# Threshold attention and an ELU feed-forward: the first 45 attention steps as one list of timed jobs

## The chip, the core and the metric

The kernel runs on one core of a Trainium2 chip. The metric is the device time of one execution in microseconds; the kernel before takes 1319.03 us (median of 3 runs, 1318.7 to 1320.56). Everything is float32. The engines are named as in the profile: PE (TensorE), DVE (VectorE), ACT (ScalarE), POOL (GpSimd), SP (the queue that issues most DMAs). Each engine runs its own instructions in the order in which the program emits them; a semaphore holds an instruction back until its inputs are there and the buffer that it writes is free. So the order of emission, engine by engine, is the schedule, and it is what this change alters.

## The reference

```python
# q, k, v: (8, 8, 576, 64); tau = 0.02; w_in (512, 2048); w_out (2048, 512)
scores = q @ k.T / 8
thresh = max(scores, axis=-1) - tau
scores = where(scores >= thresh, scores, -1e9)
attn = softmax(scores)
x = (attn @ v).transpose(0, 2, 1, 3).reshape(4608, 512)
h = x @ w_in
g = where(h > 0, h, exp(min(h, 0)) - 1)
out = g @ w_out
```

## The kernel before

**Steps.** Attention is done in pairs of heads: 32 pairs (4 to a batch entry). A pair has five steps, `steps[n] = (pr, i)`: i = 0 to 3 are 128 query rows of both heads, i = 4 (`NC`) is the last 64 rows of both heads in one tile. A step computes scores on PE (L283), the negated row maximum on DVE (L293, L321), a threshold on POOL (L325), the exponential on ACT (L335), the masked product with its row sum on DVE (L344), sum and reciprocal on DVE (L350, L351), and the normalized weights `w` on POOL (L317). The weights are then turned, so that keys lie on partitions: either by PE transposes (L354) and ACT copies (L370), in three parts (nine transposes of 128x128; six where i = 4), or "in squares": DVE transposes 32x32 blocks (L428), and two DMAs by way of DRAM put the blocks in place (L457, and `fetch`, L465). After i = 1 and after i = 4 the product with v follows (`values`, L489 and L494) and a copy of it (`values_out`, L611).

**Three loops.** The change concerns steps 0 to 44. They are emitted by three loops, in which the order is written out by hand.

- Loop 1 (L780), steps 0 to 19. PSUM holds three score tiles of one head each (two banks each) and two single banks (`t`). A step's transposes are emitted within the next step, and scores of the next step before its own second mask. Dummy transposes of the identity (`spare`, L374, counts at L793 and L825) are put ahead of the real ones. Six 512-column pieces of the feed-forward's weights are converted on the way from a double-width integer form: each needs a shift (DVE, L167), an add (POOL, L176), two activations (ACT, L156, L181) and a product (DVE, L189). In all there are 32 pieces.
- Loop 2 (L874), steps 20 to 34, with new PSUM pools: two score tiles, two banks for the feed-forward (`f`), two for `t`. Two pieces of weights are converted in each step until all are there. The feed-forward of the first 512 tokens (two chunks c of 256) is put between, in halves: a half is four matmuls, which the trace shows as eight instructions of 256 columns (`ffn1`, L652) or four of 512 columns (`ffn2_plain`, L692). A unit of `ffn1` (two halves, one bank) is followed by an exponential (ACT, L659), a subtraction (POOL, L662) and a product (DVE, L666), after which its bank is free. `SHARES` (L868) says how many halves a step takes at four points. A unit is taken only when the weight pieces that it needs are converted (`needs`, L731). The units are pushed at the end of step 21 (L949), so the first halves are emitted in step 22. After step 34 the loop turns that step's weights on PE, finishes the open unit and the open values (L953 to L956).
- Loop 3 (L1046), steps 35 to 44, with new PSUM pools again: three banks for `f`, two score tiles, one bank for `t` (L960). Here all weights are turned in squares, the halves are given by `QUOTA` (L1041), and DVE and POOL also prepare sums of the weight blocks for what follows. The SBUF pool of the early stage (`wstage`) is closed first and its space reused (`late`).

After step 44 comes the rest of the kernel, from pair 9 on: attention in wider PSUM tiles together with a feed-forward that uses fewer products (L541, L588 to L601, L1149, L1289), ordered by an agenda of jobs with times (`at`, `until`, L1098 to L1116), in which the table `MOVED` (L19) adds an offset in microseconds to a job's time. That agenda sorts the emission only; nothing on the chip waits for such a time. The rest of the kernel is not changed, except for where its three `f` banks are allocated.

The lines that decide loop 2's turning and banks, for reference:

```python
for name, bufs in (("s", 2), ("f", 2)):
...
    SHARES = ((1, 1, 1, 1), (0, 1, 1, 0), (1, 1, 1, 0), (0, 1, 1, 0), (1, 1, 1, 0))
...
            if steps[n - 2] == (NPAIR - 1, NB - 1):
                push_ffn(0)
...
        turn(*steps[SWITCH - 1])
        finish_units(ffn_halves(len(pending)), ALL)
        behind(*steps[SWITCH - 2])
        behind(*steps[SWITCH - 1])
```

Of the kernel before, what the change touches and what calls it, by code (L numbers as in the profile page):

```python
# [19 lines left out]
    'f0.0': -2.08, 'f1.0': -0.13, 'f1.1': 0.2, 'f10.0': 0.05, 'f11.0': -0.04, 'f12.1': 0.12, 'f13.1': -0.5,  # L20
    'f14.0': 0.02, 'f15.1': -0.06, 'f16.0': 0.04, 'f16.1': 0.69, 'f16.2': -0.14, 'f17.0': -0.28, 'f18.1': 0.12,
    'f2.0': -5.54, 'f2.1': -0.25, 'f2.2': 0.7, 'f20.1': -1.03, 'f21.0': 0.13, 'f22.1': -0.19, 'f23.0': 0.08,
    'f23.1': 2.72, 'f23.2': 0.07, 'f25.0': 0.39, 'f26.0': -0.08, 'f26.1': 0.42, 'f3.0': 0.35, 'f5.0': -0.32,
    'f5.1': 4.32, 'f6.1': -0.54, 'f7.0': -0.01, 'f9.0': 0.35, 'f9.1': 1.94, 'fbound0': -0.14, 'fbound1': 0.93,
    'fbound4': -0.36, 'fe00': 0.1, 'fe10': 0.37, 'fe11': 0.3, 'fe20': -0.6, 'fexp00': 0.1, 'fexp20': 0.25,
    'fexp31': 0.12, 'ffetch0': 1.19, 'ffetch1': -0.24, 'ffetch2': -0.52, 'ffetch3': -0.65, 'fkcopy': -0.11,
    'floadk': -2.59, 'floadq': 2.51, 'fm00': -3.15, 'fm01': -0.49, 'fm11': -2.07, 'fm20': 1.6, 'fm21': -0.43,
    'fmask00': 1.48, 'fmask01': -0.63, 'fmask10': 0.68, 'fmask11': 0.02, 'fmask30': -0.16, 'fmask31': 0.36,
    'fmask4': 0.2, 'fmax00': -0.03, 'fmax01': -0.65, 'fmax10': 0.91, 'fmax11': 0.5, 'fmax20': -0.99,
    'fmax21': -0.15, 'fmax30': 0.04, 'fmax31': -0.17, 'fmax4': 0.36, 'fnorm01': 0.83, 'fnorm10': -0.23,  # L30
    'fnorm11': -0.44, 'fnorm20': 1.68, 'fnorm31': -0.75, 'fout1': 0.83, 'fsum0': 0.21, 'fsum2': 0.33,
    'fsum3': 0.21, 'fturn0': 0.21, 'fturn2': 0.46, 'fturn3': -1.27, 'fturn4': -3.36, 'fx0': -0.43, 'fx10': 3.03,
    'fx11': 2.86, 'fx2': 1.4, 'fx3': 0.53, 'fx6': -1.72, 'fx8': -0.33, 'fx9': 1.95, 's13.0': -0.93,
    's13.1': 0.11, 's13.2': 0.73, 's13.3': 1.36, 's15.1': -0.14, 's17.3': -1.92, 's19.0': 0.23, 's19.1': 1.66,
    's21.0': 0.22, 's23.0': 1.98, 's23.1': 4.28, 's23.2': 2.4, 's25.1': -0.53, 's25.2': 1.32, 's25.3': 0.43,
    's27.0': -2.01, 's3.0': -0.77, 's3.2': 0.37, 's5.0': -2.21, 's7.0': 0.39, 's9.0': -3.16, 's9.1': -0.03,
    'sbound0': 0.06, 'sbound1': 0.6, 'sbound3': 0.33, 'sbound4': -0.31, 'sexp00': 0.32, 'sexp01': -0.15,
    'sexp10': -0.99, 'sexp11': -0.09, 'sexp20': 0.5, 'sexp30': -1.71, 'sexp31': -0.33, 'sexp4': 0.82,
    'sfetch0': -0.75, 'sfetch3': -0.18, 'sfetch4': 0.31, 'sloadk': -1.81, 'sm31': 0.19, 'smask11': 0.49,
    'smask20': -0.39, 'smask21': -0.03, 'smask30': -0.19, 'smask31': 0.34, 'smax10': -4.94, 'smax11': -0.3,  # L40
    'smax20': 0.07, 'smax21': 0.74, 'smax30': 0.68, 'smax4': 0.21, 'snorm00': 0.1, 'snorm01': -0.01,
    'snorm10': 0.08, 'snorm21': -0.13, 'snorm30': 0.24, 'snorm31': 1.3, 'snorm40': 0.68, 'sout0': -1.7,
    'sout1': -0.49, 'sprep0': 0.21, 'sprep1': -0.32, 'ssum3': 0.21, 'ssum4': 0.35, 'sturn0': 1.44, 'sturn1': 0.3,
    'sturn2': -0.07, 'sturn3': 0.1, 'sturn4': -1.49, 'sx0': -0.87, 'sx1': -0.05, 'sx10': 0.8, 'sx11': -0.5,
    'sx2': -1.66, 'sx3': 0.47, 'sx4': -2.3, 'sx5': 1.3, 'sx6': 1.26, 'sx8': 4.1, 'sx9': -0.98,
# [4 lines left out]
def kernel(  # L50
# [85 lines left out]
    progress = [0, 0]  # L136

    def load_w(ahead=2):
        i = progress[0]
        if i >= len(pieces) or i >= progress[1] + ahead:  # L140
            return
        progress[0] += 1
        src, dst, j, n = pieces[i]
        rows = src[j * P : (j + 1) * P]
        if src.dtype == FP32:
            nc.sync.dma_start(dst, rows[:, n : n + WN])
            return
        st = staged[i] = wstage.tile([P, WN, 2], U32, name="wst", bufs=4)
        nc.sync.dma_start(st.rearrange("p n w -> p (n w)"), rows.bitcast(U32)[:, 2 * n : 2 * (n + WN)])
# [8 lines left out]
    def convert_top(i):  # L158
        convert_shift(i)
        convert_sign(i)  # L160


# [5 lines left out]

    def convert_sign(i):
        pass  # L170
# [13 lines left out]
    def convert_end(i):  # L184

        progress[1] = i + 1
        if i in staged:
            sign, top = staged.pop(i)[:, :, 1].bitcast(I32), tops.pop(i).bitcast(FP32)
            nc.vector.scalar_tensor_tensor(pieces[i][1], top, 0.0, sign, ALU.max, ALU.mult)  # L189
# [5 lines left out]
    def load(pr, parts=("qm", "km", "v"), shared=False, queue=nc.sync):  # L195
# [13 lines left out]
        if "v" not in parts:  # L209
            return  # L210
# [38 lines left out]
    spare = []  # L249
    e_both, e_next = att.tile([P, 2, 2, HALF], FP32, name="e", bufs=1), [0]  # L250
# [49 lines left out]
    def masks(pr, i, hs):  # L300
        st = open_steps[pr, i]
        cs = slice(hs[0], hs[-1] + 1)
        if hs[0] == 0:
            st["w"] = wpool[0].tile([P, 2 * S], FP32, name="w")
# [33 lines left out]
    def mask_of(pr, i, h):  # L338
        st = open_steps[pr, i]
        if h == 0:  # L340
            st["w"] = wpool[0].tile([P, 2 * S], FP32, name="w")
# [81 lines left out]
    def turn_squares(pr, i):  # L423
        w = open_steps.pop((pr, i))["w"]
        x = late["x"].tile([P, NT, NCH, T], FP32, name="x", bufs=2)
# [279 lines left out]
    def push_ffn(g):  # L705
        if g:
            return
        for c in range(PLAIN):
            units.extend((ffn1, (c, u)) for u in range(NU))
            units.extend((ffn2_plain, (c, i, p)) for p in range(NFT // 4) for i in range(2))  # L710
# [7 lines left out]
    def behind(pr, i):  # L718
        if i in (1, NB - 1):
            values(pr, 0 if i == 1 else 1)()  # L720
        if i == NB - 1 and (pr + 1) % NPAIR == 0 and pr + 1 < NP:
            push_ffn(pr // NPAIR)
# [13 lines left out]
    def ffn_halves(n):  # L736
        after = []
        while n and (pending or units):
            if not pending:
                if needs(*units[0]) > progress[1]:  # L740
                    break
# [14 lines left out]

    with tc.manual_schedule():
        load(0, ("qm",))  # L760
        nc.sync.dma_start(tau_sb, tau.to_broadcast([P, 1]))
        load(0, ("km",), queue=nc.scalar)
        load(0, ("v",))
        load(1)


        def idle(n):
            rt = psum["t"].tile([P, NC, P], FP32, name="rt", tag="rt")
            for _ in range(n):
                transpose(rt[:, 0], ident)  # L770

        idle(28)
        prep_q(0)
        prep_k(0)
        read_tau()
        copy_k(0)
        copy_q(0)
        scores(0, 0, [0, 1])
        out_values = None
        for n in range(per_seq):  # L780
            pr, i = steps[n]
            hs = heads_of(i)
            x = progress[1]
            if n:
                normalize(*steps[n - 1], [0])
                turned = turn_parts(*steps[n - 1])
            max_of(pr, i, 0)
            exp_of(pr, i, 0)
            bound_of(pr, i, 0)

            first_scores = n > 2 and i in (2, NB - 1)
            if n and not first_scores:
                spare.append(6 if pr else 9)  # L793
                copies = turned[0]()
            if len(hs) == 2:
                max_of(pr, i, 1)
            if n and len(heads_of(steps[n - 1][1])) == 2:
                normalize(*steps[n - 1], [1])
            if len(hs) == 2:
                exp_of(pr, i, 1)  # L800
                bound_of(pr, i, 1)
            if out_values:
                out_values()
            if n and not first_scores:
                copies()

            if i == NB - 1 and n + 1 < per_seq:
                convert_top(x)
                convert_add(x)
                convert_abs(x)  # L810
                convert_rest(x + 1)
            elif i == 0 and n:
                convert_end(x)
                load_w()
            elif i == 1 and pr:
                convert_sign(x)
                convert_add(x)
            elif i in (2, 3):
                (prep_q if i == 2 else prep_k)(pr + 1)
                if i == 2:  # L820
                    scale_q(pr + 1)
                (copy_q if i == 2 else copy_k)(pr + 1)
            mask_of(pr, i, 0)
            if n and not first_scores:
                spare.append(8 if pr else 11)  # L825
                turned[1]()()
            elif not n:
                idle(16)
            if n + 1 < per_seq:
                scores(*steps[n + 1], heads_of(steps[n + 1][1]))  # L830
            if n:
                for part in turned[0 if first_scores else 2 :]:
                    part()()
            if len(hs) == 2:
                mask_of(pr, i, 1)
            reciprocal_of(pr, i, hs)
# [33 lines left out]
    with tc.manual_schedule():  # L870
        carried = []
        for _ in range(2):
            load_w(4)
# [685 lines left out]
```

## Time and profile before

| | us |
|---|---|
| median of 3 runs | 1319.03 |
| profiled execution, its own time | 1320.34 |
| its span, first to last instruction | 1318.6 |
| PE busy in the span | 1298.9 |
| DVE, POOL, ACT busy in the span | 1012.1, 805.2, 559.5 |
| start of the scores of step 0 | 8.12 |
| start of the scores of step 20 | 98.34 |
| start of the scores of step 22 | 113.55 |
| start of the scores of step 35 | 220.22 |
| start of the scores of step 44 | 288.84 |
| first PE instruction of the rest (L588) | 296.2 |

The span is counted from the first instruction. Busy times of PE are modelled: a matmul that waits inside the pipeline counts as busy, so gaps are better seen between the starts of neighbouring matmuls. The granted clock is that of PE, 1.00 being full speed. In the chain of waits each row is a stretch of the chain that ended last, with its start, its length, and the engine and line that filled it; "issue" is time in which the engine waited for nothing that the profile shows.

### The profile page before, as it was taken

Reading aid. Unit: us, or ns where it says so; the run is one execution under the profiler, and the core shown is the slowest. Engines: PE = TensorE matmul, PEld = TensorE weight load, DVE = VectorE, ACT = ScalarE, POOL = GpSimd, SP = SyncE. Lnnn points to the kernel's source line nnn. Section 1 sums busy time; section 2 is a strip of 40 time slices with the busy share of each in tenths; the row PEclk is TensorE's granted clock in tenths of the full one; section 3 lists DMA queues with packets and bytes.
Section 4 is the critical chain, followed back from the end, with each engine's and each line's share of the span. In section 5 each row is a group of like instructions: output and inputs, shape, how many; then the busy total and the mean of one; then the engine's idle time right before and its main releaser. Section 6 shows DMA issues by size and latency. Waiting matters only on the chain.

```text
span 1318.6 us, 22013 instructions
## 1 busy us (share of the span) xinstructions
PE 1298.9 (99%) x6980; PEld 1011.0 (77%) x6980; DVE 1012.1 (77%) x2195; ACT 559.5 (42%) x1219; POOL 805.2 (61%) x1186
## 2 busy tenths in 40 slices
PE   8999999999999999999999999999999999999998
PEld 7666756647778777777878777878777787888886
DVE  6877775988888988898898979897889882545534
ACT  5676664225353444444443535252526250422320
POOL 4657774768657665767475747584768463624533
PEclk9998999999999999999999999999999999999999
DMA  6255452788897989898889888989889775221221
GB/s 120 61 107 161 136 143 57 220 241 241 222 257 221 259 214 245 214 260 232 240 216 256 239 234 224 259 240 245 234 235 258 216 214 185 93 72 60 93 60 32
DMA packets 322595, 247.76 MB, mean 188 GB/s; under 512 B 208688, under 2 KB 284464, under 8 KB 322480
## 3 DMA queue, kind: packets, MB, share of 16 engines
q1 hardware_dynamic: 320112, 246.07, 68.6%
q8 instruction: 55, 0.90, 0.3%
q10 hardware_dynamic: 2368, 0.30, 0.2%
q14 instruction: 60, 0.49, 0.1%
HBM read 161.81 MB, written 84.48 MB: 187 GB/s over the span
## 4 chain that ended last, share of the span: by engine, by line
PE 93%; DVE 3%; DMA 1%; ACT 1%; issue 1%; SPq 1%; POOL 0%; ACTq 0%; DVEq 0%
PE f L1289 29%; PE f L1149 28%; PE sc L541 8%; PE sc L601 7%; PE rt L354 4%; PE sc L283 4%; PE f L652 4%; PE f L692 3%; PE pv L494 3%; PE sc L593 1%; PE sc L588 1%; DMA there<-x 1%; PE pv L489 1%; DVE x L428 1%; SPq L457 0%
## 5 line engine op out<-in xcount | busy, mean ns | idle before, releaser
L317 POOL TENSOR_SCALAR w<-w,rs 128x576 f32<-128x576 f32 x196 | 169.1, 871 | 85.6 <-DVE rs L351 75.5
L548 DVE TENSOR_REDUCE mx<-sc 128x1 f32<-128x576 f32 x207 | 148.3, 750 | 35.3 <-PE sc L541 32.4
L558 ACT ACTIVATE w<-sc,mx 128x576 f32<-128x576 f32 x115 | 83.0, 740 | 114.6 <-DVE mx L548 96.8
L1149 PE MATMUL f<-xt,sw 128*128 128x256 f32 x512 | 123.8, 384 | 0.8 <-ACT xt L611 0.5
L1149 PE MATMUL f<-xt,w_in_sb 128*128 128x256 f32 x512 | 122.3, 381 | 0.3 <-ACT w L1163 0.3
L554 POOL TENSOR_SCALAR th<-mx,ntau 128x2 f32<-128x2 f32 (+1 forms) x115 | 34.3, 298 | 137.8 <-DVE mx L548 137.8
L1149 PEld LDWEIGHTS f<-xt,w_in_sb 128*128 128x128 f32 x512 | 96.1, 190 | 16.0 <-ACT w L1163 3.2
L1149 PEld LDWEIGHTS f<-xt,sw 128*128 128x128 f32 x512 | 93.7, 190 | 18.2 <-ACT xt L611 0.9
L541 PE MATMUL sc<-kT,qT 64*128 64x512 f32 (+4 forms) x736 | 107.5, 423 | 0.0
L1149 PE MATMUL f<-x,w_in_sb 128*128 128x256 f32 x448 | 106.1, 379 | 1.4 <-ACT g L1210 1.4
L1289 PE MATMUL f<-w_out_sb,g 128*128 128x256 f32 x448 | 107.1, 382 | 0.0
L541 PEld LDWEIGHTS sc<-kT,qT 64*128 64x128 f32 x736 | 80.8, 186 | 34.2 <-issue 16.8
L1289 PE MATMUL f<-w_out_sb,s 128*128 128x256 f32 x448 | 107.0, 382 | 0.0
L1289 PE MATMUL f<-t,s 128*128 128x256 f32 x448 | 105.8, 379 | 0.0
L428 DVE STREAM_TRANSPOSE x<-w 128x512 f32<-128x512 f32 (+2 forms) x143 | 96.6, 709 | 10.6 <-POOL w L317 10.3
L562 DVE SCALAR_TENSOR_TENSOR w<-sc,th,w 128x576 f32<-128x576 f32 x115 | 89.8, 811 | 11.4 <-ACT w L558 9.2
L1236 POOL TENSOR_TENSOR s<-g 128x256 f32<-128x256 f32 x104 | 80.4, 779 | 29.4 <-PE f L1289 20.1
L1149 PEld LDWEIGHTS f<-x,w_in_sb 128*128 128x128 f32 x448 | 85.0, 190 | 13.4 <-ACT g L1210 1.8
L1289 PEld LDWEIGHTS f<-w_out_sb,g 128*128 128x128 f32 x448 | 84.1, 190 | 12.9 <-issue 0.7
L1289 PEld LDWEIGHTS f<-t,s 128*128 128x128 f32 x448 | 85.1, 190 | 11.6
L1289 PEld LDWEIGHTS f<-w_out_sb,s 128*128 128x128 f32 x448 | 84.2, 190 | 12.3
L317 POOL TENSOR_SCALAR e<-e,rs 128x576 f32<-128x576 f32 x92 | 68.5, 749 | 35.5 <-DVE rs L351 34.2
(193 smaller groups left out, 2858.7 us busy)
## 6 DMA issues: line engine op xcount, KB each, us to landing
there<-x SPq DMA_DIRECT2D x408, 144.0 KB, 3.7
wTb<-there SPq DMA_DIRECT2D x52, 576.0 KB, 6.5
wTa<-there SPq DMA_DIRECT2D x50, 576.0 KB, 4.9
sw<-win_sums SPq DMA_DIRECT2D x62, 384.0 KB, 4.2
t<-wout_sums SPq DMA_DIRECT2D x45, 512.0 KB, 5.7
qm<-in_q_dram SPq DMA_DIRECT2D x128, 72.0 KB, 4.5
vm<-in_v_dram SPq DMA_DIRECT2D x64, 128.0 KB, 3.2
wst<-in_moe_w_in_dram SPq DMA_DIRECT2D x16, 512.0 KB, 4.4
```

Source lines behind the costliest of these rows:

```text
L283: nc.tensor.matmul(scs[h][:, a, :HALF], qs[r], kT[r, k0 : k0 + HALF], start=True, stop=True)
L317: nc.gpsimd.tensor_scalar(wv, wv, st["rs"][:, h : h + 1], 1.0, ALU.mult, ALU.mult)
L354: nc.tensor.matmul(dst, src, ident, is_transpose=True, skip_group_check=True)
L428: nc.vector.transpose(x[:, :, c0 : c0 + nc_], src.rearrange("p (c g n) -> p g c n", c=nc_, n=T))
L541: on_banks(nc.tensor.matmul(o, qT[r, i * P : (i + 1) * P], kT[r, k0 : k0 + n], start=True, stop=True, skip_group_check=True), o)
L548: on_banks(nc.vector.tensor_reduce(st["mx"][:, h : h + 1], st["sc", h], axis=AX.XY if i == NC else AX.X, op=ALU.max, negate=True), st["sc" ...
L558: on_banks(nc.scalar.activation(st["e", h], st["sc", h], AF.Exp, bias=st["mx"][:, h : h + 1]), st["sc", h])
L562: on_banks(nc.vector.scalar_tensor_tensor(st["e", h], st["sc", h], st["th"][:, h : h + 1], st["e", h], ALU.is_ge, ALU.mult, accum_out=st[" ...
L601: on_banks(nc.tensor.matmul(o, vm[:, h, c], parts[part][:, g0:g1, h * (NC + 1) + c], start=False, stop=(c == NC - 1), skip_group_check=Tru ...
L1149: nc.tensor.matmul(loc["banks"][place], left[:, j], right[:, j], start=(begins and j == 0), stop=(j == 1), skip_group_check=True)
L1236: engine.tensor_tensor(o, x, y, op)
L1289: nc.tensor.matmul(place(m), lhs, rhs, start=(begins and v == 0), stop=(v == RU - 1), skip_group_check=True)
```

## The change

The three loops are replaced by one set of jobs. `task(x, t, key, f, *needed)` registers a job under a name, with a nominal time `t` plus the offset that `MOVED` has for its key, and with the jobs that must be emitted before it. The jobs are then emitted in the order of their times, each one's needs first. Nominal times start at `begin[n]`: 5.0 us a step up to step 20, 7.2 us from there on. The offsets (582 new entries) lie between -7.18 and +9. In detail:

- every instruction group of a step is a job of its own: scores; maximum, exponential, threshold, mask and normalization per head; each part of a turn and each copy out of it; shift, add, two activations and product of a weight piece; loads; each half of the feed-forward and each of its three follow-ups.
- steps 0 to 34 have three `w` buffers (`WBUFS`) where they had two.
- seven weight pieces are placed in steps up to 19 (there were six), then two per step as before.
- the first chunk's units are pushed once the first values of pair 3 are copied out, the second chunk's with its second values. Halves are tried from step 20 on, by the same `SHARES` and `QUOTA`, and still only where the weight pieces are converted.
- at step 20 the PSUM pools change as before. At step 35 they do not: steps 35 to 44 run with two `f` banks and two `t` banks. The three `f` banks of the rest are allocated after step 44, from the closed pools.
- the turn of step 33 is done in squares (`SQUARES`, by the entry `"sq33": 2.27`), with two `x` tiles in the early pool; its nine PE transposes and three ACT copies go, three DVE transposes, four DMAs out and one DMA in take their place.
- the numbers of dummy transposes are the same. The turn of step 34, the open unit and the open values are no longer emitted in one block ahead of step 35.

```diff
+    "half0b0": 2.6, "half0b2": 0.03, "half0b4": -1.89, "half0c0": -0.35, "half0c1": 3.13, "half0c2": -1.05,
...
-    progress = [0, 0]
-
-    def load_w(ahead=2):
-        i = progress[0]
-        if i >= len(pieces) or i >= progress[1] + ahead:
-            return
-        progress[0] += 1
+    progress = [0]
+
+    def load_w(i):
...
+    WBUFS = 3
...
-            st["w"] = wpool[0].tile([P, 2 * S], FP32, name="w")
+            st["w"] = wpool[0].tile([P, 2 * S], FP32, name="w", bufs=WBUFS if wpool[0] is wstage else None)
...
-        x = late["x"].tile([P, NT, NCH, T], FP32, name="x", bufs=2)
+        x = late.get("x", wstage).tile([P, NT, NCH, T], FP32, name="x", bufs=2)
...
-        for n in range(per_seq):
...
-        for n in range(per_seq, SWITCH):
...
-    for name, bufs, stack in (("f", 3, ctx), ("s", 2, banks), ("t", 1, banks)):
-        psum[name] = stack.enter_context(tc.tile_pool(name=f"ps_{name}2", bufs=bufs, space=PSUM))
...
+    SQUARES = [*range(SWITCH, MIDDLE), *(n for n in range(per_seq + 2, SWITCH) if MOVED.get(f"sq{n}", 0.0) > 1.0)]
+    made = {}
+
+    def task(x, t, key, f, *needed):
+        made[x] = [t + (MOVED.get(key, 0.0) if key else 0.0), len(made), f, needed, False]
+
+    def do(x):
+        job = made[x]
+        if not job[4]:
+            job[4] = True
+            for y in job[3]:
+                if y:
+                    do(y)
+            job[2]()
...
+        begin = [5.0 * min(n, per_seq) + 7.2 * max(0, n - per_seq) for n in range(MIDDLE + 4)]
...
+        def room_for(pool, release):
+            while len(taken[pool]) >= 2:
+                taken[pool].popleft()()
+            taken[pool].append(release)
...
+        slots = [(n, x) for n in range(NB - 1, SWITCH)
+                 for x in range(steps[n][1] in (NB - 1, 1) if n < per_seq else 2)][: len(pieces)]
...
+        def half():
+            if not pending:
+                if not units or needs(*units[0]) > progress[0]:
+                    return
...
+                back = ("turned", n - (2 if last_ else WBUFS)) if n >= WBUFS else None
...
+                def run_out(pr=pr, part=part, got=got):
+                    got[0]()
+                    if (pr, part) == (NPAIR - 1, 0):
+                        push_ffn(0)
+                    elif (pr, part) == (NPAIR - 1, 1):
+                        push_ffn(1)
...
+            if n >= per_seq:
+                for x, c in enumerate(SHARES[n % NB] if n < SWITCH else QUOTA[n % NB]):
+                    for y in range(c):
+                        u = ((2.4, 6.4) if last_ else (1.2, 4.0, 4.8, 5.2))[x]
+                        task(("half", n, x, y), t + u, f"half{x}{k}", half)
...
+        for x in sorted(made, key=lambda x: made[x][:2]):
+            do(x)
...
-        for n in range(SWITCH, MIDDLE):
...
+        early_tasks()
...
-        ends = [bank() for _ in range(3)]
+        ends = []
...
         banks.close()
+        psum["f"] = ctx.enter_context(tc.tile_pool(name="ps_f2", bufs=3, space=PSUM))
+        ends.extend(bank() for _ in range(3))
```

## The prediction

> **What bounds the kernel now.** I read the busy shares of the page first, then windows over the changed stretch (up to 296 us; what follows keeps its instructions), then the chain of waits and the starts of PE's instructions. Of PE, the page says:
>
> ```profile
> PE 1298.9 (99%) x6980; PEld 1011.0 (77%) x6980; DVE 1012.1 (77%) x2195; ACT 559.5 (42%) x1219; POOL 805.2 (61%) x1186
> ```
>
> 19.7 us of idle PE in the whole span would leave little to win. The windows (loop 1; steps 20 and 21; the dense part of loop 2; the rest of loop 2 with the passage to loop 3; most of loop 3) show another picture:
>
> ```profile
> core 0: us, PE busy (x) PEld busy (x) DVE busy (x) ACT busy (x) POOL busy (x), PEclk, DMA share, GB/s
> 8.00:98.00 90.00, 87.35 (x631) 63.70 (x632) 72.23 (x175) 61.77 (x133) 51.33 (x97) 1.00 0.44 94
> 98.30:113.50 15.20, 12.74 (x52) 6.10 (x50) 9.20 (x22) 8.62 (x21) 10.81 (x13) 0.78 0.45 142
> 113.50:177.20 63.70, 63.70 (x332) 44.93 (x331) 52.05 (x105) 44.78 (x88) 50.67 (x60) 1.00 0.62 162
> 177.20:198.70 21.50, 21.01 (x92) 10.64 (x91) 14.64 (x31) 14.19 (x30) 15.03 (x17) 1.00 0.32 101
> 198.70:242.60 43.90, 42.98 (x209) 29.86 (x209) 27.20 (x59) 17.04 (x36) 22.74 (x33) 1.00 0.32 85
> 242.60:296.00 53.40, 51.75 (x198) 27.43 (x198) 46.63 (x106) 11.96 (x21) 37.85 (x56) 1.00 0.86 246
> ```
>
> The reader should see three things. In 98.3 to 113.5 PE does 3.4 matmuls per us, against 5.2 in the next row, and its clock falls to 0.78, which is half speed for some 6.8 of 15.2 us. In 198.7 to 242.6 DVE is busy 62% of the time, because attention is held up while the feed-forward runs; in the next window it is 87%. And in loop 1 (first row) DVE is the fullest engine with real work, 80%, since part of PE's time there is dummies. The chain of waits between 97 and 115 us shows what happens after step 20:
>
> ```profile
> 101.79 0.65 ACT e L335
> ...
> 102.53 0.59 DVE w L344
> ...
> 103.51 0.72 PE sc L283 x2
> ...
> 104.25 1.83 PE sc L283 x6
> 106.08 1.58 PE pv L489 x2
> 107.65 4.23 PE pv L494 x16
> ```
>
> The scores of step 21 wait for a mask of step 20 (PE idle 2.18 us in the timeline), then run slowly: 16 value instructions of 320 columns take 4.23 us, where the same 16 take 2.30 at 40.7 us. After 113.5 the chain is PE without a break to 177 (`1.73 PE f L652 x8` between scores of 1.17): PE bounds loop 2 there.
>
> **PE's own work, steps 20 to 44.** Prices from the chain: scores 1.17 us (1.0 where i = 4); a half 1.73; turning nine transposes 0.98 and six 0.65 (0.109 from start to start); values with their first product 2.5 for part 0 (122.3 to 124.8) and 3.1 for part 1 (146.6 to 149.7). Counted from the program: 20 x 1.17 + 5 x 1.0 = 28.4; 64 halves x 1.73 = 110.7; turns of steps 19 to 34, 12 x 0.98 + 4 x 0.65 = 14.4; values 5 x 2.5 + 5 x 3.1 = 28. Sum 181.5. The stretch lasts 296.2 - 98.3 = 197.9. So PE has 16.4 us to spare. Where: steps 20 and 21, 15.2 elapsed against 7.2 of work, 8.0; between starts at 241.3 (1.1), 249.5 (1.5) and 295.3 (0.6), scores waiting for masks around the passage to loop 3, 3.2; 182.5, 0.6; the rest in pieces under 0.5.
>
> **The change, part by part.**
> - *Feed-forward from step 20.* I put the jobs in order by their printed times and needs, and counted PE's list. Step 20 gets 4 halves, step 21 two, step 22 two. Six halves, 6 x 1.73 = 10.4 us, now lie where 8.0 us were lost, so PE is never short there and the clock should hold. Steps 20 and 21 get longer (8.9 and 8.7), later ones shorter. Gain up to 8.0.
> - *What it costs later.* Halves wait for weight pieces, two per step. With the earlier start the units catch up with the pieces: step 24 has one half, 26 none, 28 one, 34 two. There PE has 3.7, 5.3, 6.4 and 4.5 us of work. DVE's part of a step is: maxima 2 x 0.75, masks 2 x 0.89, sum and reciprocal 0.33, two pieces 2 x 1.1, on average 0.6 of a product at 0.68 and 0.4 of a transpose of q or k at 0.77: 6.5 us, about 4.6 where i = 4. PE loses 6.5 - 5.3 = 1.2 at step 26, 0.9 at step 24, and up to as much, say 0.5 each, at 22, 30, 32 and 35: 4 us. None of it if PE's denser neighbours lend their time, 7 if each of these steps loses its 0.9 to 1.2.
> - *No block at step 35.* The waits of 3.2 us have no cause of their own left, and halves are spread over steps 33 to 44. Gain up to 3.2.
> - *Two banks instead of three in steps 35 to 44.* Not seen before at this density. With two, the third unit after waits for the first unit's product. Before, the lag from a unit's last matmul to the end of its product was 2.2 to 5.4 us in loop 2 with two banks, 2.9 to 7.1 in loop 3 with three. One unit plus scores covers 3.46 + 1.17 = 4.6. Bounds: 0 (lag as at 2.9), and 7 units x (7.1 - 4.6) = 17. Eight of the thirteen lags up to 238 us lie under 3.5 us, two over 4.6, so I take 2.5.
> - *Step 33 in squares.* PE loses nine transposes, 0.98. ACT loses three copies (0.59 + 0.59 + 0.27). DVE gains 1.41 (the row `DVE x L428 x3` of the chain), SP five issues, landing in 3.7 us in the page; SP is not on the chain in loop 2 and the values that need it come three steps later. Gain 1.0; if that cover failed, values of pair 6 would be late by one landing, 3.7.
> - *Third w buffer, loop 1 in jobs.* DVE waited in loop 1 for exponentials 8.3 us, scores 4.8, thresholds 1.2, a w buffer 1.1: 15.4 in all, above a floor of 72. The buffer takes the 1.1. DVE's own order in loop 1 hardly differs (maxima, then masks); with three score tiles the scores still wait for the first mask, and PE carries the same dummies: per pair 4 x 1.17 + 1.0 of scores, 4.6 real and 4.6 dummy transposes, 5.6 of values: 20.5 of 22.5 us (starts of scores at 29.4 and 51.9). So the gain lies between 0 and 4 x 2.0 = 8; a loss would need a new wait, and the needs leave each engine's order near the old one. I take 4.
> - *Everything else* (loads as jobs, a seventh early piece, banks of the rest allocated after step 44) at nothing: SP has been far ahead, and PE's first product of the rest follows 1.2 us after L588. If those banks come free late, it costs under 1.
>
> Sum: old slack 16.4, and 1.0 less work; new slack 4 (sparse steps) + 2.5 (banks) + 3 (pieces as before) = 9.5. Gain in steps 20 to 44: 17.4 - 9.5 = 7.9; loop 1: 4. In all 12 us. The profiled execution took 1320.34 us with a span of 1318.6, 1.3 above the median; a saving carries over one to one: 1319.0 - 12 = 1307.
>
> **Two rules weighed.** The Trainium skill (TensorE: Matmul & The Clock Gate, The HAM clock gate) says that the clock falls to half after an idle window of about 3.4 us. By it, no gap that I foresee in the sparse steps (1.1 us) would cost clock. Here the row decides: the clock halved for 6.8 us after a gap of only 2.2 us amid short ones, and stayed full after 1.5 us. So a sparse step that stalls 2 us more than I think would cost 3.4 beyond the stall; these steps have no dummies. The skill's front page (Trainium Kernel Development and Optimization, Performance Expectations) says that matmul busy is a bad metric and weight-load busy a good one. By the latter, 119 of 197.7 us, 40% of the stretch would be free, 79 us; by the starts of matmuls it is 16.4. The dense row shows why I hold to the starts: 71% weight loads (44.93 of 63.70) with no gap in the chain.
>
> **Rivals.**
> - *More is recovered* (1297 to 1301): PE dense throughout, loop 1 at 20.5 a pair: 16.4 + 1.0 + 8 = 25, less 3 to 7. For it: DVE and POOL are under 85% in nearly every window. Against: the pieces' pace makes sparse steps whatever the order. 14%.
> - *The slack only moves* (about 1318): the sparse steps lose what steps 20 and 21 win, 8, and loop 1 gives nothing. For it: total halves and pieces are fixed. Against: it needs 8 us in sparse steps, twice my count. 9%.
> - *Two banks throttle the second chunk* (about 1324): if lags in steps 35 to 39 run to 7.1 us, as three did around 241 to 254, seven units lose 17, and 12 + 2.5 - 17 is a loss of 3 to 5, with a clock drop. It decides from a mean lag of 4.6 + 14.5 / 7 = 6.7 us. For it: POOL's 2.7 us of extra sums and DVE's square transposes stand between there. Against: those lags had a third bank to hide in, and nothing hurried them. 8%.
>
> **How the numbers follow.** The main case, 1301 to 1314, has 60%; between 1314 and 1316 another 9%. A measurement can tell about 0.2%, 2.6 us, from no change. Faster: 60 + 14 + 9 = 83%; same 9%; slower 8%. The range goes from 1297 to 1318.
>
> **What would show it.** Right: clock 1.00 in all windows between 8 and 296 us; feed-forward matmuls ahead of the scores of step 21; step 22 later than now, about 116 us less loop 1's gain, but L588 at about 284; loop 1 shorter by a few us. Wrong: gaps over 1 us ahead of L652 released by the product L666 (banks), gaps ahead of scores in steps 24 to 34 (sparse), a half clock anywhere in between, or the rest, from L588 to the end, longer than its 1022 us.

## The result and the profile after

The changed kernel takes 1312.98 us (median of 6 runs, 1311.99 to 1314.63), beside 1319.69 for the kernel before in the same comparison (6 runs): a ratio of 0.9949 with a 95% interval of 0.9937 to 0.9962, 6.7 us less. The prediction was 1307, 12 us less, in a range of 1297 to 1318. The direction was right, and the gain a little over half of what was forecast.

The profiled execution has a span of 1311.1 us, 7.5 less than before. Its windows, cut at the same steps as before (loop 1; steps 20 and 21; 22 to 29; 30 to 32; 33 to 37; 38 to 44):

```profile
core 0: us, PE busy (x) PEld busy (x) DVE busy (x) ACT busy (x) POOL busy (x), PEclk, DMA share, GB/s
8.00:98.00 90.00, 88.76 (x633) 63.75 (x633) 71.26 (x173) 62.28 (x132) 51.35 (x97) 1.00 0.46 105
98.20:116.90 18.70, 18.11 (x99) 13.43 (x98) 13.83 (x28) 11.93 (x26) 12.77 (x15) 1.00 0.40 117
116.90:172.80 55.90, 54.57 (x286) 36.23 (x285) 50.72 (x100) 43.97 (x87) 49.36 (x59) 1.00 0.65 170
172.80:192.80 20.00, 20.00 (x91) 10.29 (x90) 15.25 (x33) 13.68 (x28) 13.88 (x19) 1.00 0.43 97
192.80:234.20 41.40, 40.66 (x194) 27.59 (x193) 29.39 (x67) 13.66 (x27) 22.97 (x34) 1.00 0.51 147
234.20:289.00 54.80, 53.19 (x209) 28.35 (x207) 45.23 (x99) 13.34 (x25) 38.83 (x57) 1.00 0.85 229
```

The clock is 1.00 in every row, and steps 20 and 21 now hold 99 matmuls in 18.7 us where they held 52 in 15.2. DVE is at 71% in steps 33 to 37 (29.39 of 41.40), where it stood at 62%. In the chain of waits at step 20, PE stands where masks and slow values stood:

```profile
97.14 0.84 DVE w L425 x2
...
99.14 1.10 POOL w L398
...
100.28 0.87 PE rt L435 x6
101.16 6.91 PE f L733 x32
108.06 1.17 PE sc L364 x8
```

Those 32 matmuls are the four halves of step 20, ahead of the scores of step 21. Who PE waited for between 8 and 290 us (microseconds in total, times, longest):

```profile
PE f L733 <- DVE g L747: 1.5, 2, 0.8
PE rt L435 <- POOL w L398: 1.5, 3, 0.6
PE rt L435 <- issue: 1.0, 4, 0.3
PE sc L364 <- DVE pos L200: 0.9, 1, 0.9
PE sc L669 <- ACT ot L778: 0.7, 1, 0.7
```

No scores wait for a mask any more. In the kernel before they did:

```profile
PE sc L283 <- DVE w L344: 2.7, 2, 2.2
PE sc L283 <- DVE w L309: 2.3, 2, 1.3
```

The first two rows after are new: a feed-forward matmul waits for the product that frees its bank, and transposes wait for the normalization on POOL.

Starts of scores, the first PE instruction of the rest, and where the clock was at half, from one profiled execution each; medians and ratios to the kernel before from the timed runs:

| kernel | step 20 | step 33 | step 35 | rest | half clock, us | median | ratio (interval) |
|---|---|---|---|---|---|---|---|
| before | 98.3 | 198.7 | 220.2 | 296.2 | 6.8 at 104.7 | 1319.69 | |
| after | 98.2 | 192.8 | 207.3 | 289.0 | none | 1312.98 | 0.9949 (0.9937 to 0.9962) |
| before, gap filled | 98.1 | 195.1 | 216.7 | 292.6 | none | 1317.02 | 0.9982 (0.9975 to 0.9989) |
| before, early halves | 98.4 | 198.7 | 220.3 | 296.2 | 3.4 at 182.5 | 1322.37 | 1.0020 (1.0013 to 1.0026) |
| before, no dummies | 98.3 | 195.3 | 216.8 | 292.8 | 3 times 3.4, loop 1 | 1316.86 | 0.9981 (0.9974 to 0.9987) |
| before, half the dummies | 95.3 | 195.4 | 216.9 | 292.9 | 6.8 at 100.7 | 1316.93 | 0.9977 (0.9968 to 0.9985) |
| before, two banks | 98.5 | 198.3 | 219.8 | 296.9 | 6.8 at 103.2 | 1320.21 | 1.0003 (0.9995 to 1.0012) |
| after, late halves | 98.3 | 196.7 | 211.7 | 293.1 | 3.4 at 105.3 | 1318.43 | 0.9991 (0.9984 to 0.9997) |
| after, no offsets | 101.7 | 201.6 | 216.7 | 309.3 | 6.8, 3.4, 3.4 | 1331.85 | 1.0090 (1.0077 to 1.0104) |
| after, step 33 on PE | 98.4 | 193.0 | 208.7 | 293.9 | 3.4 at 237.8 | 1316.52 | 0.9973 (0.9963 to 0.9983) |
| after, two w | 98.4 | 193.0 | 207.8 | 288.9 | none | 1312.70 | 0.9950 (0.9937 to 0.9962) |
| after, no dummies | 103.6 | 198.1 | 212.5 | 294.4 | 3.4, 6.8, 6.8, loop 1 | 1317.83 | 0.9992 (0.9986 to 0.9999) |
| after, half the dummies | 97.6 | 192.3 | 206.8 | 288.5 | none | 1311.45 | 0.9935 (0.9923 to 0.9948) |
| after, loop 1 by hand | 94.8 | 193.2 | 207.8 | 288.7 | 3.4 at 99.1 | 1312.90 | 0.9949 (0.9935 to 0.9962) |

Each ratio is to runs of the kernel before on the same chip, whose median was 1319.5 to 1320.2 in the experiments. From the rest to the end every kernel but the one without offsets takes 1022.0 to 1022.7 us, that one 1023.1.

### The profile page after: what moved, and what is told of

Same layout as the page of the kernel before. It is cut to its first block, busy times and chain, and to the rows that moved or that the text cites. A ratio compares the mean times of both kernels' runs of the same rounds, so it can differ in the third digit from the quotient of the medians.

```text
span 1311.1 us, 21958 instructions
## 1 busy us (share of the span) xinstructions
PE 1294.9 (99%) x6971; PEld 1008.1 (77%) x6971; DVE 1016.4 (78%) x2198; ACT 559.8 (43%) x1216; POOL 801.0 (61%) x1186
## 4 chain that ended last, share of the span: by engine, by line
PE 92%; DVE 3%; DMA 2%; POOL 1%; issue 1%; SPq 1%; ACT 0%; ACTq 0%; DVEq 0%; POOLq 0%
PE f L1369 29%; PE f L1229 28%; PE sc L622 8%; PE sc L682 7%; PE f L773 4%; PE rt L435 4%; PE sc L364 3%; PE f L733 3%; PE pv L575 2%; PE sc L674 1%; PE sc L669 1%; PE pv L570 1%; DVE w L425 1%; DMA vd<-in_v_dram 1%; DMA there<-x 1%
## 5 line engine op out<-in xcount | busy, mean ns | idle before, releaser
L398 POOL TENSOR_SCALAR w<-w,rs 128x576 f32<-128x576 f32 x196 | 163.8, 843 | 82.0 <-DVE rs L432 65.8
L509 DVE STREAM_TRANSPOSE x<-w 128x512 f32<-128x512 f32 (+2 forms) x146 | 98.2, 706 | 13.2 <-POOL w L398 12.8
```

The costliest lines, as they stand in the source:

```text
L398: nc.gpsimd.tensor_scalar(wv, wv, st["rs"][:, h : h + 1], 1.0, ALU.mult, ALU.mult)
L509: nc.vector.transpose(x[:, :, c0 : c0 + nc_], src.rearrange("p (c g n) -> p g c n", c=nc_, n=T))
```

## The experiments

**Where the gain is: clock, early halves, order.** My theory after the result was that the filled steps 20 and 21 are nearly the whole gain; the rival, that the order as a whole is.

The kernel before with the first chunk's halves allowed from step 20:

```diff
             if n == per_seq:
                 for x in now:
                     convert_rest(x)
+                push_chunk(0)
...
-                push_ffn(0)
+                push_chunk(1)
```

> The kernel before with the first chunk's units pushed before step 20 in place of after step 21; nothing else. Theory (the gain of the change is the filled steps 20 and 21): clock 1.00 throughout, the start of the rest 5 to 7 us earlier, total lower by 5 to 7 us, nearly the whole gain of the change. Rival (the gain comes from the order as a whole, banks kept, blocks dissolved): 0 to 2 us, since the halves that come earlier are missing later, where the weight pieces set the pace.

Measured: slower, ratio 1.0020; in the profiled execution step 33 and the rest start within 0.1 us of where they did. My theory fell. PE waits and the chain around 180 us (start, length, engine and line):

```profile
PE sc L283 <- DVE w L344: 3.5, 2, 2.2
```

```profile
181.63 0.72 PE sc L283 x2
...
182.38 2.17 PE sc L283 x6
184.54 1.52 PE pv L489 x2
186.07 2.30 PE pv L494 x16
```

The same wait of 2.2 us, here with 3.4 us of half clock, stands before the scores of step 31 instead of step 21, and a second wait of 1.3 us within those of step 25. The halves that moved to steps 20 and 21 are missing in the steps that the weight pieces starve, and there the hand-written order leaves PE without work while it waits for a mask. That is the prediction's second rival, the slack only moves, in this order. It even grows: this execution starts the rest at the same 296.2 with 1.7 us less lost to the clock, and its timed executions with a granted clock of 0.999 or 1.000 took 1319.1 to 1320.0 us, where those of the kernel before with 1.000 took 1316.9 to 1317.4.

The kernel before with dummies in the gap:

```diff
+            if n == per_seq + 1:
+                idle(20)
             scores(*step, hs)
```

> The kernel before with 20 dummy transposes (20 x 0.109 = 2.2 us) ahead of the scores of step 21, in the gap in which PE waited for a mask; they do no work. If the clock's fall is a cost by itself, it stays at 1.00 and the total falls by 3 to 3.4 us (half of 6.8 us). If the clock costs nothing because what follows waits for something else, the total stays within 1 us.

Measured: clock 1.00, the rest 3.6 us earlier, where 3 to 3.4 was expected; by the timed runs 2.4 us (0.9982). The dummies do nothing but hold the clock, so the clock is a cost of its own. Why the median shows less than the profile is told under the hardware below.

The changed kernel without the early halves:

```diff
-            if n >= per_seq:
+            if n >= per_seq + 2:
                 for x, c in enumerate(SHARES[n % NB] if n < SWITCH else QUOTA[n % NB]):
...
-        while pending:
+        while pending or units:
             half()
```

> The changed kernel with the feed-forward's halves tried from step 22 on instead of step 20; all else as changed. Filling steps 20 and 21 by itself gave nothing in the kernel before (the early halves were missing later and the clock fell there instead). Theory now: what counts is the clock, and the slack that is not clock only moves. Then this kernel loses 3.4 us if the clock falls around step 21, and under 1.5 us if it doesn't. Rival (early halves are worth their 8 us, and only the hand-written order lost them again): 6 to 8 us slower, start of the rest near 296.

Measured: the gap before the scores of step 21 is back, with 3.4 us of half clock:

```profile
103.37 1.97 PE L364 MATMUL sc<-kT,qT 64*128 64x288 f32 x8 [2.10 <-DVE w L425]
```

The rest starts 4.1 us later than in the changed kernel. The ratios differ by 0.0042, 5.5 us; the profiled execution is the second fastest of the 21. Of the 4.1, half of 3.4 is clock; 2.4 is not. So the early halves are worth 2.4 us in the jobs' order, whose offsets were left as they are, and in the order by hand they cost about 2: both theories were too simple.

The changed kernel with the jobs at their nominal times:

```diff
-        made[x] = [t + (MOVED.get(key, 0.0) if key else 0.0), len(made), f, needed, False]
+        made[x] = [t, len(made), f, needed, False]
...
-        while pending:
+        while pending or units:
             half()
```

> The changed kernel with all offsets of the first 45 steps taken as zero, so that jobs go by their nominal times; the set of steps in squares stays. If the gain is in the structure (jobs, banks kept, earlier halves): within 2 us of the changed kernel. If it is in the order that the offsets make (no sparse step in which PE stops long enough for the clock): at least one fall of the clock in loop 2 or 3 and 4 us or more above the changed kernel, at or above the kernel before.

Measured: ratio 1.0090, 19 us above the changed kernel's 0.9949. Its waits between 98 and 310 us show by what:

```profile
PE f L733 <- DVE g L747: 8.5, 5, 3.3
PE sc L364 <- DVE w L425: 2.9, 3, 2.2
```

Step 20 starts 3.5 us later, and from there to the rest it is 207.6 us in place of 190.8. These two rows and half of the 13.7 us at half clock, 6.8, add up to 18.2, where the changed kernel has 1.5, and so make up that difference. The structure alone, with its two banks, is slower than the three loops; it is the offsets, which place each product and each mask, that bring the gain.

**Banks and squares.** The kernel before with two feed-forward banks in steps 35 to 44:

```diff
-    for name, bufs, stack in (("f", 3, ctx), ("s", 2, banks), ("t", 1, banks)):
+    for name, bufs, stack in (("f", 2, banks), ("s", 2, banks), ("t", 2, banks)):
```

with three banks allocated for the rest as in the change.

> The kernel before with two feed-forward banks and two single banks in steps 35 to 44, as in the change, in place of three and one. In the changed kernel PE waits for the product that frees a bank 1.5 us in all (predicted 2.5). Theory: the hand-written order, whose product lags were 5.9 to 7.1 us in steps 38 and 39, loses more: the rest starts 1 to 4 us later. If the lags were long only because nothing hurried them: under 0.5 us. If two banks for the values help more than the third bank did: earlier.

Measured: step 35 to the rest takes 77.1 us in place of 76.0, and the waits have one new row:

```profile
PE f L692 <- DVE g L666: 0.9, 1, 0.9
```

The total can't be told from the kernel before. The product lags (from a unit's last matmul to the end of its product) of 5.9, 7.0 and 6.6 us are the same with two banks, so a short bank did not hurry them; only the second made PE wait. In the changed kernel they run up to 8.2 us in these steps, and two of 6.4 and 5.4 make PE wait, 1.5 in all.

The changed kernel with step 33 turned on PE:

```diff
-    SQUARES = [*range(SWITCH, MIDDLE), *(n for n in range(per_seq + 2, SWITCH) if MOVED.get(f"sq{n}", 0.0) > 1.0)]
+    SQUARES = [*range(SWITCH, MIDDLE)]
```

> The changed kernel with step 33 turned on PE like its neighbours. By the prediction's price PE has 0.98 us more to do in a stretch in which it is dense: the rest starts 1.0 us later. If squares were hidden anyway or their DMAs hold up the values: 0, or below.

Measured: the rest 4.9 us later, the ratio 0.0024 higher, 3.2 us. PE in the timeline (start, length, operation, and in brackets the idle time ahead and what ended it):

```profile
211.76 0.91 PE L570 MATMUL pv<-wTb,vd 128*128 128x384 f32 x2 [1.06 <-ACT wTb L451]
...
236.64 2.62 PE L364 MATMUL sc<-kT,qT 64*128 64x288 f32 x8 [1.46 <-DVE w L425]
```

More than nine transposes: with step 33 on PE the values of pair 6 also get another nominal time (the formula asks for squares), are emitted earlier, and wait for ACT's copies; later a gap of 1.5 us brings 3.4 us of half clock. So 0.98 us is the price of the transposes at most as a part of this, and what the squares alone are worth stays open, since the offsets were not set anew for the other set of squares.

**The third w buffer and loop 1.** The changed kernel with two w buffers:

```diff
-    WBUFS = 3
+    WBUFS = 2
```

> The changed kernel with two w buffers in steps 0 to 34 instead of three (a job's need moves from the turn three steps back to that two steps back, so masks may be emitted later). Loop 1 did not get shorter with the third buffer, so if dummies or the chain under them hold it, step 20 still starts at 98 to 98.5 and the rest within 1 us. If the third buffer is what lets PE stay dense in steps 22 to 33 (94.6 us from step 20 to 33 against 97.0 in the kernel before with the gap filled): step 33 later by 2 us or more.

Measured: no difference. The instructions of every engine keep their order, and all starts of the table agree within 0.5 us. The third buffer is worth nothing here.

The dummies in loop 1, in both kernels (here the changed one; in the kernel before the four counts at L793 and L825):

```diff
-                        spare.append((8 if x else 6) if n >= NB - 1 else (11 if x else 9))
+                        spare.append(0)
```

> The changed kernel without the dummy transposes of loop 1 (the leading 28 and 16 at the start stay). Theory: PE with its dummies is what holds a pair of loop 1 at 22.5 us; 4.6 us of PE go per pair, so the pair falls to some 19 to 20 us (the floor of DVE is 18) and the total by 8 to 12 us, if the clock stays at 1.00. Rival, latency of the chain maximum, exponential, mask: dummies only fill PE's waits, a pair stays at 22 to 22.5 and the total within 2 us. Third possibility: the clock falls to half in loop 1, and the kernel gets slower by 5 or more.

> The kernel before without the dummy transposes of loop 1. Theory as for the changed kernel: the pair falls from 22.5 to 19 to 20 us and the total by 8 to 12 us, if the clock holds. Rival: within 2 us. Since the hand-written order has the third w buffer's wait and some waits for exponentials more, a gain that is 2 or more us smaller than in the changed kernel would say that the jobs' order of loop 1 is worth something that the dummies hide.

Measured: the clock falls three times in each. In the changed kernel loop 1 gets 5.4 us longer, with 8.5 us lost to the clock (half of 3.4 + 6.8 + 6.8); in the kernel before it stays as long, with 5.1 lost, and where its clock held, a pair takes 21.6 us (step 13 at 67.6, step 18 at 89.2). By its profile the kernel before gains its time at step 21, where the same gap of 2.2 us did not bring the clock down in this execution.

With half of them:

```diff
-                        spare.append((8 if x else 6) if n >= NB - 1 else (11 if x else 9))
+                        spare.append((4 if x else 3) if n >= NB - 1 else (6 if x else 4))
```

> The changed kernel with about half the dummy transposes of loop 1 (3 and 4 in place of 6 and 8; 4 and 6 in place of 9 and 11). Without any, a pair of the kernel before took 21.6 us where the clock held, against 22.5 with all, but the clock fell three times. Theory: PE with dummies is the bound by a small margin, and the chain through DVE lies 0.9 below; with half of them a pair takes 21.6 to 22, the clock holds and the total falls by 2 to 4 us against the changed kernel. Rival: the clock falls at least once in loop 1 all the same, and the total is equal or worse.

> The kernel before with about half the dummy transposes of loop 1 (3 and 4; 4 and 6). In the changed kernel the same halving brought step 20 forward by 0.6 us (98.2 to 97.6). Theory: under the dummies lies a chain (maximum, exponential, mask, normalization, transposes) that neither order shortens; then step 20 starts at 95 to 98 here too, and the clock holds in loop 1. If step 20 comes at 95 or earlier, the hand-written order of loop 1 is the better one once the dummies are thinned. Whether the clock falls at step 21 is open; it costs up to 3.4.

Measured: the clock holds in loop 1 in both. In the kernel before a pair takes 21.6 us (4.56 + 3.98 + 4.53 + 4.69 + 3.81) and step 20 comes 3.0 us earlier; in the changed kernel a pair takes 22.3 and step 20 comes 0.6 earlier. What PE waits for between 30 and 98 us, first in the changed kernel with all its dummies, then with half:

```profile
PE rt L435 <- issue: 0.8, 3, 0.3
```

```profile
PE rt L435 <- POOL w L398: 3.0, 9, 0.5
PE sc L364 <- DVE w L425: 1.5, 3, 0.5
PE rt L435 <- issue: 0.8, 3, 0.3
```

With all of them PE waits 0.8 us in 68 (2.4 in the order by hand, for ACT's copies): dummies included, it all but fills loop 1, at 22.5 us a pair in either order. Half of the dummies are 21 transposes a pair, 2.3 us of PE at 0.109 each, but the pair gets only 0.2 us shorter in the jobs' order and 0.9 in the order by hand: there the chain beneath shows. So the jobs' order of loop 1, with these offsets, is the worse of the two once the dummies are thinned, and with all of them it can't be seen.

The two best parts together: the jobs of steps 0 to 19 emitted in the order by hand, half the dummies, and the jobs by their times from step 20.

```diff
+        do(("sc", 0))
+        for n in range(per_seq):
+            pr, i = steps[n]
...
+            do(("max", n, 0)), do(("exp", n, 0)), do(("th", n, 0))
...
         for x in sorted(made, key=lambda x: made[x][:2]):
             do(x)
```

> The changed kernel with the jobs of steps 0 to 19 emitted in the order of the kernel before, and about half its dummy transposes (3 and 4; 4 and 6); from step 20 on the jobs by their times. If loop 1 and the rest add up: step 20 at 95.3 as in the kernel before with half its dummies, 190.8 us from there to the rest as in the changed kernel, clock 1.00, total 2.5 to 3 us below the changed kernel and 9 to 10 below the kernel before. If jobs of steps 18 to 20 that the change had interleaved matter, or the clock falls at step 20 (it did at 100.7 in the kernel before with half its dummies, where PE waited for a mask): equal to the changed kernel or up to 3 us above.

Measured: step 20 at 94.8, 3.4 us earlier than in the changed kernel, and the total the same (0.9949). All of it is given back within step 20. PE and POOL in the timeline:

```profile
94.76 1.24 PE L364 MATMUL sc<-kT,qT 64*128 64x288 f32 x8
98.96 1.49 PE L435 MATMUL rt<-ident,w 128*128 128x128 f32 x6 [2.96 <-POOL w L398]
```

```profile
96.36 1.29 POOL L252 TENSOR_TENSOR wtop<-wtop,wst 128x512 int32<-128x512 int32 x1 [3.62 <-ACT wst L240]
97.62 1.28 POOL L398 TENSOR_SCALAR w<-w,rs 128x576 f32<-128x576 f32 x1
```

POOL stands 3.6 us before the add of a weight piece, and the normalization of step 19 is queued behind it: my order by hand converts six pieces in loop 1, the jobs' times count on seven, so the seventh's add comes first in the sorted list and waits. PE is idle 2.96 us, and the clock falls for 3.4. The second outcome of the expectation, with a cause that the graft itself brought in; whether the two parts add up without it was not run.

## Why the prediction was right and where it was not

- *Feed-forward from step 20, gain up to 8.0.* The mechanism is there: clock 1.00, step 20 takes 9.8 us (8.9 forecast), step 21 8.9 (8.7), step 22 starts at 116.9 (116 forecast, less what loop 1 would gain). From step 20 to the rest it is 190.8 us in place of 197.9, a gain of 7.1 against 7.9. That the two are so near is in part luck: 3.4 of the 7.1 is clock that this execution of the kernel before lost and some others did not.
- *New slack, 9.5 forecast, 190.8 - 180.5 = 10.3 found*, but otherwise made up, so that the sum came out by luck. The sparse steps 22, 24, 26, 30, 32 and 35 take 1.9 us more than PE's priced work (4 forecast); banks cost 1.5 (2.5 forecast, from lags of which one, not two, lay over 4.6 us up to 238); pieces in between the other 6.9 (3 forecast). With early halves the order by hand takes 81.6 us from step 22 to 33, against 75.9; 1.7 of the difference is clock, and 4.0 is not. I had priced the steps by their work and not by the order within them.
- *Loop 1, gain 4 forecast, 0.1 found.* This is the term that was mis-sized, and with it a third of the 12 us. I read DVE as loop 1's bound with PE's dummies as filler, priced PE at 20.5 of 22.5 us a pair, and took half of the 2 us as gain. But PE was all but full: it waits 0.8 us in 68. Of the 2 us, the starts of PE's instructions from 30.7 to 53.2 us put 1.3 between neighbouring transposes that stand further apart than 0.109; what fills the rest was not worked out. With the dummies unchanged there was next to nothing to win, and with half of them this order wins 0.6 us, not 4.
- *No block at step 35, up to 3.2.* From step 33 to the rest 96.2 us against 97.5: 1.3, of which the squares' 0.98 would be most if the price is right. The waits for masks (2.3) are gone, and the waits for banks (1.5) came in their place.
- *Third w buffer, the 1.1 us.* Nothing: with two buffers the time is the same (0.9950).
- *The rest.* 1022.1 against 1022.4 us, as forecast.

The forecast of 11.9 us (7.9 + 4) stands against 7.5 in the span; the timed runs show 6.7, as the profiled execution of before lay among its longer runs (1320.34 us). Of the 7.2 us by which the rest starts earlier, 3.4 to 3.6 is the clock that no longer falls (the filled gap), 2.4 the early halves in an order that can use them, 1.3 lies after step 33. By the timed runs the clock is less of it: 2.4 us (0.9982), and 4.3 from there to 0.9949.

## What to carry to other kernels

When an engine that holds the bound is padded with dummy work, test the padding before the order: as long as it fills the engine, no order beneath it can be seen, good or bad. Work moved forward into a gap is worth only what the places that it leaves can do without; look for the next starved stretch, and put a price on the clock of its longest wait. And a schedule's pieces don't add up across a seam: check what the sorted list puts first where two orders meet.

## What the runs showed of the hardware

A gap of 2.2 us on PE does not always bring the clock down. The same gap before step 21 (2.1 to 2.2 us) was followed by 6.8 us at half clock in three profiled executions (before, half the dummies, two banks), by 3.4 in one (late halves), and by none in the kernel before without dummies. The falls seen within the kernels last 3.4 or 6.8 us, which costs 1.7 or 3.4.

The traces show a fixed window. Between two changes of the clock there is always a whole number of times 3.413 us: 98.99 in the kernel before (29 times), 13.65 and 20.48 without dummies (4 and 6), 37.55 and 30.72 without offsets (11 and 9). The edges lie elsewhere in each execution: the clock falls at 104.69 in the kernel before and at 103.22 with two banks, whose program is the same up to there. Cut at these edges, first the kernel before, then the one without dummies:

```profile
core 0: us, PE busy (x), PEclk, DMA share, GB/s
101.27:104.69 3.42, 1.22 (x7) 1.00 0.23 95
104.69:111.51 6.82, 6.82 (x24) 0.50 0.47 155
```

```profile
99.31:102.72 3.41, 1.92 (x12) 1.00 0.85 192
102.72:106.13 3.41, 2.70 (x11) 1.00 0.42 169
```

In the first the whole gap lies in one window, in the second the edge at 102.72 divides it, 1.5 and 0.7 us. So part of a window without work is enough, and where the edges lie decides with it. How large the part must be does not come out: 1.46 us within one window brought a fall in the changed kernel with step 33 on PE, and these 1.5 did not. The Trainium skill (TensorE: Matmul & The Clock Gate, The HAM clock gate) describes such a free-running window, but asks for a whole idle one; the prediction weighed that rule and kept the shorter gap as dangerous.

The times of the kernel before lie in three heaps accordingly. Of its 73 runs beside the first experiments, 10 lie at 1316.9 to 1317.4, all with a granted clock of 1.000; 26 from 1318.5 to 1319.1, with 0.997 or 0.998; and 37 from 1319.5 to 1320.7, most with 0.996. The kernel with the gap filled lies between 1316.73 and 1317.52, all 21 runs, where the first heap is. That is why its median gains 2.4 and not 3.6: some runs of the kernel before lost less to the clock than the profiled one.
